# Grouped attention and a gated MLP on one core: V and U of batch 0 in one accumulation each, and a second order of the start-up's words

## The chip, the cores and the metric

One NeuronCore of a Trainium2 chip. The time is device microseconds of one launch. Each kernel is executed several times, and the median is given; one execution was profiled by the hardware profiler, and its trace is what the views are taken from.

## The reference

Eight batches; each is independent of the others but for the weights.

```python
# q 8x16x384x64, k and v 8x4x384x64 (four query heads share a k/v head)
attn = softmax(q @ k.T / 8) @ v            # by batch and head
x = attn, heads joined                      # 8 x 384 x 1024
h = relu(x @ w_in)                          # 1024 -> 1024
u, v = h[..., :512], h[..., 512:]
v = (v - mean(v)) / sqrt(var(v) + 1e-6)     # over the 512
v = w_spatial @ v + b_spatial               # over the 384 positions
out = (u * v) @ w_out                       # 512 -> 1024
```

## The kernel before

The work is cut into small steps, each with a short name, and the order of the steps is written out by hand as lists of words (RAMP, START, STEADY, LAST). A word is a step, its indices and its batch: in START a word without marks is batch 0, `+` is one batch on, `++` two, `+++` three; in STEADY and LAST `'` is one batch back. Each word issues its instructions on whatever engines they need, and every engine runs its own instructions strictly in the order in which the words issue them. So one list sets at once the order of TensorE (PE), VectorE (DVE), ScalarE (ACT), GpSimd (POOL) and of the DMA queues of SP and POOL. Waits between engines are put in by the framework from the buffers that are written and read.

By batch, the words are:

- **Loads** (SP's queue): `lk`, `lq0`, `lq1`, `lv` bring k, the two halves of q (768 KB each) and v in fp32. For batch 0 they are cut finer (`lqj`, `lqd`, `lkg`). The fp32 buffers are single (pool `ld`, one buffer by tag): a load of the next batch waits until the casts of the one before have read the buffer. `wv0`, `wv1`, `wu0`, `wu1` (L137) and `wo` (L144) load and convert the weights from POOL's queue; `wv` is the V half of w_in's columns, `wu` the U half, 0 and 1 the first and last four of its eight row blocks. `ws` (L150, L151) loads the spatial weight and bias, `cws` casts them on POOL (L157, L160), `tws` (L166) turns the weight by a DMA transpose.
- **Casts** to fp16: `ck`, `cq0`, `cq1`, `cv` on POOL (L184, L247, L197); in batch 0 also pieces on VectorE (`cqjv`, `cqv`, `ckv1`) and ScalarE (`cka0`).
- **Turns**: k and q, and later x, must lie with their head dimension on the partitions. In batches 0 and 1 `Q`, `K`, `Tp` do this on TensorE (L292, L278, L378) with a copy back by VectorE (L297, L283, L379); from batch 2 on (for x from batch 1 on) `tk`, `tq`, `T` are DMA transposes in SP's queue (L263, L269, L368).
- **Attention**: `s0` to `s17` are score products (two matmuls of 512 columns into a pair of PSUM banks, L315), `e0` to `e17` their exponentials on ScalarE (L329), `X` the products with v (24 matmuls, L342), `N` the division by the row sums (VectorE, L356, L357), which gives a half of an x tile (the half of the heads that X's first index names).
- **MLP**: `V` is the V half of x @ w_in for one tile of 128 positions (8 matmuls of 512, L113), then relu on VectorE (L434) into v_r; `S` its mean and variance (L447, L448), `rs` 1/sqrt on ScalarE (L452, L453), `vn` the normalised tiles (L461), `p` the spatial product (L113, bias added at L492), `U` the U half for 128 of its columns (8 matmuls of 384), gated at L505, `O` the output product with copy (L525) and store (L533).
- `w` and a number: so many matmuls of 128 columns on a cleared tile (L303), results unused.

PSUM has eight banks. A helper hands out the bank, or the even pair, that has been unused for longest, in the order of the words; a step that gets a bank still being read waits for that reader.

In batch 0 before the change, V and U are split in START. `A0` to `A2` multiply the first four row blocks of w_in (the first half of the heads) and VectorE copies the result to SBUF (L414); the later `V0` to `V2` multiply the last four, add the kept part (L436) and take the relu of the sum in SBUF (L437). `H0` to `H3` and `U0` to `U3` do the same for U (copy L423, add L503, gate L505 from the sum). All other batches do V and U in one accumulation of eight matmuls. `gate_v` and `gate_u` take the split branch only where a kept part exists.

START covers batch 0, most of batches 1 and 2 and the loads of batch 3. STEADY is played for batches 3 to 7, LAST ends the work.

Of the kernel before, what the change touches and what calls it, by code (L numbers as in the profile page):

```python
# [17 lines left out]
def kernel(  # L18
# [622 lines left out]
    def play(b, text):  # L641
# [8 lines left out]
    RAMP = """  # L650
        lqj00 lkga0 lqj01 lqd01 lt lkg1 lqd10 lv lqd11"""
    START = """
        w28 cqjv00 cka0 Qj00 w4 Ka0 w5 cqjv01 Qj01 w7 cqp011 wv0 cqv010 s0 s2 cv wv1 lk+ lq0+ Qh01 cqv100 ckv1
        cqv111 s1 e0 lq1+ ws s3 lv+ w9 s5 e2 ck+ e1 cqv101 s4 e5 e4 w6 cq0+ cqv110 s7 wu0 Q10 K1 cq1+ cws Q11
        s8 e7 e3 wu1 tws s10 lk++ s6 s9 e6 e8 lq0++ e10 X00 X01 e9 lq1++ lv++ N00 s11 N01 e11 s13 X02 e13 N02
        s12 cv+ Tp00 X10 wo e12 N10 Tp01 K0+ A0 Tp10 Q12 s14 e14 A1 V0 X11 Tp02 s15 N11 s16 K1+ A2 s17 e16
        Tp11 Q00+ S0 e15 e17 V1 X12 N12 s1+ Q10+ Q01+ Tp12 e1+ s0+ s9+ e0+ S1 e9+ s10+ ck++ H0 Q11+ Q02+ V2
        s2+ e10+ S2 e2+ s11+ rs s3+ e3+ H2 s4+ vn e11+ cq0++ H1 e4+ X00+ cq1++ tk++ N00+ p1 X10+ s5+ tq0++
        tq1++ N10+ T0+ p0 H3 e5+ U0 s12+ e12+ s7+ Q12+ U1 p2 s13+ s14+ e7+ p3 e13+ cv++ X01+ N01+ e14+ U3 s6+
        lk+++ U2 s17+ X11+ e17+ e6+ N11+ lq0+++ T1+ s8+ V0+ O4 e8+ X02+ N02+ s2++ S0+ e2++ lq1+++ s15+ O5 s0++  # L660
        e0++ s1++ O0 e15+ s16+ e16+ O2 lv+++ e1++ O1 V1+ O3 s11++ X12+ e11++ s9++ ck+++ e9++ N12+ T2+ S1+
        s10++ X00++ N00++ e10++ s14++ cq0+++ X10++ s3++ s5++ N10++ e5++ s4++ e4++ V2+ e3++ cq1+++ s13++ e14++
        tk+++ s12++ tq0+++ s8++ tq1+++ e13++ X01++ S2+ rs+ e12++ T0++ e8++ vn+ N01++ s7++ X11++ N11++ e7++ p1+
        p2+ p0+ V0++ cv+++ s15++ s17++ s6++ e6++ U0+ e15++ X02++ s16++ N02++ S0++ e17++ e16++ T1++ U1+"""
    STEADY = """
        s2 s1 e2 s0 e0 U2'' X12' p3'' N12' lq0+ cq0+ e1 lk+ s11 lq1+ e11 U3'' s9 tq0+ s10 s4 e9 e10 O0'' X00
        N00 ck+ V1' X10 S1' e4 s5 s3 T2' e5 lv+ e3 N10 O1'' V2' S2' s14 s13 s12 e13 T0 e12 O2'' O3'' X01 e14
# [45 lines left out]
```

## Time and profile before

| | before |
|---|---|
| median of 8 executions | 255.5 us (254.25 to 259.04) |
| the profiled execution | 255.13 us, span 253.0 us |
| TensorE busy | 237.0 us (94%), mean granted clock 0.993 |
| VectorE, ScalarE, POOL busy | 173.9, 143.6, 46.8 us |
| DMA | 47.2 MB, mean 187 GB/s |
| busy of PE / DVE / ACT / POOL, 20 to 30 us | 8.57 / 9.15 / 4.59 / 10.00 us |
| 30 to 40 us | 8.81 / 9.12 / 6.27 / 1.33 us |
| 40 to 50 us | 9.81 / 9.60 / 6.77 / 4.71 us |
| 50 to 60 us | 7.55 / 4.36 / 3.11 / 1.86 us |

The span is the profiled execution from its first to its last instruction; the execution's own time, 255.13, holds 2.1 us around it. Busy time counts an engine's instructions without its waits. The granted clock is the share of TensorE's full speed that the throttle allowed. The DMA share is the mean busy share of the core's 16 DMA engines; in a short window it can come out above 1. In a timeline each line is a run of equal instructions: start, length, engine, code line, operation, what it writes and reads, how many, and in brackets the idle time ahead of it with what ended it. SPq lines are the issue of a DMA by SP, not its transfer.

### The profile page before, as it was taken

How to read it: one execution, taken by the hardware profiler on the slowest of the kernel's cores; microseconds unless marked ns; L12 is line 12 of the kernel's file. 1: busy time of each engine (PE TensorE's matmuls, PEld its weight loads, DVE VectorE, ACT ScalarE, POOL GpSimd, SP SyncE). 2: the span in 40 equal slices, each digit the busy share in tenths (PEclk: the TensorE clock that was granted, in tenths of full speed). 3: DMA queues.
4: the chain of work that ended last, by engine and by line, in shares of the span. 5: the costliest groups of instructions: out<-in, count | busy, mean ns of one | idle time of the engine just before them, and what ended most of it. 6: DMA issues, size and time to landing. Idle time of an engine off the chain costs nothing.

```text
span 253.0 us, 5788 instructions
## 1 busy us (share of the span) xinstructions
PE 237.0 (94%) x2395; PEld 129.8 (51%) x2395; DVE 173.9 (69%) x350; ACT 143.6 (57%) x164; POOL 46.8 (18%) x72
## 2 busy tenths in 40 slices
PE   7779798969978999999999999999999999999993
PEld 6446345434535454464545554465446454565672
DVE  2538989936648557966677667775787677776963
ACT  3984476644576784856658466748485765800000
POOL 1718800704200151002310061003300000000000
PEclk9999999988999999999999999999999999999999
DMA  6999899999794994779968798789879126220354
GB/s 207 262 271 336 128 229 295 171 230 256 247 190 93 272 156 123 192 183 283 194 192 210 209 249 167 221 160 275 217 172 168 23 44 206 87 41 0 126 210 166
DMA packets 78042, 47.20 MB, mean 187 GB/s; under 512 B 47168, under 2 KB 74176, under 8 KB 78016
## 3 DMA queue, kind: packets, MB, share of 16 engines
q1 hardware_dynamic: 74880, 43.36, 67.7%
q0 software_dynamic: 2720, 3.15, 7.5%
q8 instruction: 18, 0.29, 0.5%
q10 hardware_dynamic: 416, 0.33, 0.4%
q14 instruction: 8, 0.07, 0.1%
HBM read 25.95 MB, written 12.58 MB: 152 GB/s over the span
## 4 chain that ended last, share of the span: by engine, by line
PE 83%; DVE 6%; DMA 5%; ACT 4%; issue 1%; SPq 0%; DVEq 0%; ACTq 0%
PE banks L113 57%; PE banks L315 13%; PE banks L342 12%; ACT aT L329 4%; DMA q<-in_q_dram 2%; DMA k<-in_k_dram 1%; DMA xT<-x 1%; DVE v_r L437 1%; DVE v_r L436 1%; DVE bn L447 1%; PE banks L292 1%; DVE q L247 1%; DVE gT L505 0%; PE banks L378 0%; DVE qT L297 0%
## 5 line engine op out<-in xcount | busy, mean ns | idle before, releaser
L329 ACT ACTIVATE aT<-banks 128x1024 f16<-128x1024 f32 x144 | 137.8, 1025 | 73.1 <-PE banks L315 66.9
L113 PE MATMUL banks<-w_in,xT 128*128 128x512 f16 x192 | 46.4, 384 | 4.0 <-DMA xT<-x 2.5
L113 PE MATMUL banks<-w_out,gT 128*128 128x512 f16 (+1 forms) x196 | 48.0, 381 | 0.0
L342 PEld LDWEIGHTS <-aT 128*128 128x128 f16 x1152 | 41.0, 98 | 13.3 <-ACT aT L329 5.9
L113 PE MATMUL banks<-xT,w_in 128*128 128x384 f16 (+1 forms) x320 | 47.3, 294 | 0.1
L315 PE MATMUL banks<-qT,kT 64*128 64x512 f16 x288 | 44.5, 381 | 2.2 <-ACT aT L329 0.6
L342 PE MATMUL banks<-v,aT 128*128 128x65 f16 x1152 | 43.4, 194 | 3.0 <-ACT aT L329 3.0
L247 POOL CAST q<-q 128x768 f16<-128x768 f32 (+1 forms) x29 | 23.6, 842 | 101.9 <-DMA q<-in_q_dram 65.6
L525 DVE COPY osb<-banks 128x512 f32<-128x512 f32 x47 | 32.0, 687 | 10.4 <-PE banks L113 9.9
L113 PEld LDWEIGHTS <-w_in 128*128 128x128 f16 x320 | 25.7, 98 | 17.7 <-issue 5.9
L357 DVE TENSOR_TENSOR x<-banks,rec 128x512 f16<-128x512 f32 x48 | 33.2, 691 | 1.7
L113 PEld LDWEIGHTS <-xT 128*128 128x128 f16 x192 | 18.1, 98 | 24.8 <-DMA xT<-x 3.0
L434 DVE TENSOR_SCALAR v_r<-banks 128x512 f32<-128x512 f32 x21 | 14.5, 691 | 23.0 <-PE banks L113 23.0
L113 PEld LDWEIGHTS <-gT 128*128 128x128 f16 x196 | 17.1, 99 | 24.9 <-issue 10.0
L315 PEld LDWEIGHTS <-kT 64*128 64x128 f16 x288 | 12.1, 94 | 24.8 <-issue 19.0
L505 DVE SCALAR_TENSOR_TENSOR gT<-banks,vs 128x384 f16<-128x384 f32 x24 | 13.4, 558 | 11.7 <-PE banks L113 11.7
L492 DVE TENSOR_TENSOR vs<-banks,bias_tp 128x384 f32<-128x384 f32 x28 | 14.9, 552 | 6.6 <-PE banks L113 6.6
L113 PE MATMUL banks<-wsT,v_n 128*128 128x384 f16 x96 | 19.3, 326 | 0.0
L447 DVE BATCH_NORM_STATS2 bn<-v_r 128x6 f32<-128x512 f32 x24 | 16.5, 689 | 0.4
L356 DVE RECIPROCAL rec<-banks 128x8 f32<-128x8 f32 x48 | 9.7, 202 | 9.1 <-PE banks L342 8.0
L461 DVE TENSOR_SCALAR v_n<-v_r,mv,rstd 128x512 f16<-128x512 f32 x24 | 11.6, 540 | 0.7 <-ACT rstd L453 0.6
L113 PEld LDWEIGHTS <-v_n 128*128 128x128 f16 x96 | 8.0, 98 | 6.2 <-issue 2.3
(49 smaller groups left out, 92.2 us busy)
## 6 DMA issues: line engine op xcount, KB each, us to landing
out_dram<-osb SPq DMA_DIRECT2D x22, 512.0 KB, 3.0
q<-in_q_dram SPq DMA_DIRECT2D x14, 768.0 KB, 8.1
v<-in_v_dram SPq DMA_DIRECT2D x8, 384.0 KB, 4.0
k<-in_k_dram SPq DMA_DIRECT2D x7, 384.0 KB, 6.4
w_in<-in_moe_w_in_dram POOLq DMA_DIRECT2D x8, 256.0 KB, 6.8
q<-in_q_dram SPq DMA_DIRECT2D x8, 192.0 KB, 4.2
w_out<-in_moe_w_out_dram POOLq DMA_DIRECT2D x2, 512.0 KB, 11.7
out_dram<-osb SPq DMA_DIRECT2D x3, 256.0 KB, 2.1
```

What stands on the lines that cost most here:

```text
L113: nc.tensor.matmul(dst[c : c + cols], w[:, c : c + cols], m, start=(i == 0), stop=(i == n - 1))
L247: engine(columns(b, gp, T["q16", b, gp])[:, js, :, half, :], T["q32", b, gp][:, half, js, :].rearrange("p j (t d) -> p j t d", t=NST),)
L315: nc.tensor.matmul(banks[:, xs[half], :], T["kT", b][lo:hi, t, gp, :], rhs[lo:hi, c * 512 : (c + 1) * 512], start=True, stop=True,)
L329: nc.scalar.activation(T["aT", b, gp, c][:, t, :, :], banks[:, x : y + 1 : y - x, :], AF.Exp, scale=scale)
L342: nc.tensor.matmul(banks[:, xs[half], j * (D + 1) : (j + 1) * (D + 1)], aT[:, t, half, o : o + P], T["v16", b][:, 2 * gp + half, t, 0 : D ...
L357: nc.vector.tensor_tensor(T["x16", b, tq][:, gp], ps[:, :, :, 0:D], rec.to_broadcast([P, 2, G, D]), ALU.mult)
L434: nc.vector.tensor_scalar(v_r, banks[:, x, :], 0.0, None, op0=ALU.max)
L447: nc.vector.bn_stats(bn, T["v_r", b, st])
L461: engine.tensor_scalar(v_n, T["v_r", b, st], T["mv", b][:, st, 0:1], T["rstd", b][:, st : st + 1], op0=ALU.subtract, op1=ALU.mult,)
L492: nc.vector.tensor_tensor(vs, f32(x, S), bias_tp, ALU.add)
L505: nc.vector.scalar_tensor_tensor(T["gT", b][:, mu, :], src, 0.0, T["vs", b, mu], op0=ALU.max, op1=ALU.mult)
L525: copy(osb[:, half * 512 : (half + 1) * 512], banks[:, x, :])
```

## The change

START is replaced. Its words are the same but for these: `A0` to `A2` and `H0` to `H3` are gone, so that `V0` to `V2` and `U0` to `U3` of batch 0 take the branch of one accumulation over eight row blocks; and there are 74 matmuls of the `w` words instead of 59. The order of the other words differs from just behind `s0` on, for all batches in START. SP's queue keeps its order up to the load of batch 3's first q half, and POOL's whole queue keeps its order; on TensorE, VectorE and ScalarE instructions change places. Among the moves: `ckv1`, the VectorE cast of the second half of batch 0's k, stands behind the copies of `Q10` and `Q11` and the four q casts on VectorE (before, behind the first of the four and ahead of the copies); `s0++` and `e0++` stand ahead of `V0+` (before, behind); `lq1+++` stands ahead of `T1+`, and `lv+++` ahead of the stores. Nothing else in the file changes; STEADY and LAST are the same.

```diff
--- before.py
+++ after.py
@@ -650,18 +650,18 @@
     RAMP = """
         lqj00 lkga0 lqj01 lqd01 lt lkg1 lqd10 lv lqd11"""
     START = """
-        w28 cqjv00 cka0 Qj00 w4 Ka0 w5 cqjv01 Qj01 w7 cqp011 wv0 cqv010 s0 s2 cv wv1 lk+ lq0+ Qh01 cqv100 ckv1
-        cqv111 s1 e0 lq1+ ws s3 lv+ w9 s5 e2 ck+ e1 cqv101 s4 e5 e4 w6 cq0+ cqv110 s7 wu0 Q10 K1 cq1+ cws Q11
-        s8 e7 e3 wu1 tws s10 lk++ s6 s9 e6 e8 lq0++ e10 X00 X01 e9 lq1++ lv++ N00 s11 N01 e11 s13 X02 e13 N02
-        s12 cv+ Tp00 X10 wo e12 N10 Tp01 K0+ A0 Tp10 Q12 s14 e14 A1 V0 X11 Tp02 s15 N11 s16 K1+ A2 s17 e16
-        Tp11 Q00+ S0 e15 e17 V1 X12 N12 s1+ Q10+ Q01+ Tp12 e1+ s0+ s9+ e0+ S1 e9+ s10+ ck++ H0 Q11+ Q02+ V2
-        s2+ e10+ S2 e2+ s11+ rs s3+ e3+ H2 s4+ vn e11+ cq0++ H1 e4+ X00+ cq1++ tk++ N00+ p1 X10+ s5+ tq0++
-        tq1++ N10+ T0+ p0 H3 e5+ U0 s12+ e12+ s7+ Q12+ U1 p2 s13+ s14+ e7+ p3 e13+ cv++ X01+ N01+ e14+ U3 s6+
-        lk+++ U2 s17+ X11+ e17+ e6+ N11+ lq0+++ T1+ s8+ V0+ O4 e8+ X02+ N02+ s2++ S0+ e2++ lq1+++ s15+ O5 s0++
-        e0++ s1++ O0 e15+ s16+ e16+ O2 lv+++ e1++ O1 V1+ O3 s11++ X12+ e11++ s9++ ck+++ e9++ N12+ T2+ S1+
-        s10++ X00++ N00++ e10++ s14++ cq0+++ X10++ s3++ s5++ N10++ e5++ s4++ e4++ V2+ e3++ cq1+++ s13++ e14++
-        tk+++ s12++ tq0+++ s8++ tq1+++ e13++ X01++ S2+ rs+ e12++ T0++ e8++ vn+ N01++ s7++ X11++ N11++ e7++ p1+
-        p2+ p0+ V0++ cv+++ s15++ s17++ s6++ e6++ U0+ e15++ X02++ s16++ N02++ S0++ e17++ e16++ T1++ U1+"""
+        w28 cqjv00 cka0 Qj00 w4 Ka0 w5 cqjv01 Qj01 w7 cqp011 wv0 cqv010 s0 cv e0 Qh01 s2 wv1 lk+ e2 s1 w10
+        cqv111 s4 cqv100 e1 cqv110 cqv101 s5 lq0+ lq1+ s3 s7 ws e3 w20 lv+ ck+ cq0+ e5 wu0 cq1+ Q10 e7 Q11
+        ckv1 s8 e4 e8 K1 cws s6 wu1 s9 tws lk++ s10 e6 X00 e10 e9 s11 X01 N00 N01 Tp00 X02 Q12 s13 N02 e11 X10
+        N10 lq0++ lq1++ Tp01 s12 lv++ K1+ s14 e12 K0+ Tp10 V0 cv+ e14 wo e13 Tp02 X11 N11 ck++ s17 s16 s15 e17
+        S0 Tp11 e15 e16 V1 Q00+ X12 N12 Q10+ s1+ s0+ Tp12 e1+ s9+ Q01+ S1 e9+ s10+ e0+ V2 S2 e10+ s2+ e2+ s3+
+        cq0++ Q11+ rs s11+ s4+ X00+ vn e11+ e4+ p1 e3+ cq1++ N00+ p0 tk++ X10+ s5+ Q02+ N10+ e5+ p2 U0 s12+
+        s7+ s14+ tq0++ p3 e7+ tq1++ U2 s13+ e12+ Q12+ cv++ T0+ s6+ lk+++ e14+ e6+ U3 U1 e13+ X01+ N01+ s17+
+        lq0+++ s8+ e17+ X11+ s0++ N11+ e8+ e0++ V0+ lq1+++ O2 T1+ X02+ N02+ O0 s1++ lv+++ s2++ s15+ e2++ e1++
+        O4 O5 s16+ e16+ O1 O3 ck+++ s11++ s9++ e15+ X12+ e11++ e9++ N12+ V1+ cq0+++ S0+ s10++ e10++ s5++ s3++
+        X10++ S1+ e5++ X00++ N10++ s4++ T2+ N00++ cq1+++ s14++ e14++ V2+ tk+++ S2+ s13++ s7++ e4++ e3++ s8++
+        e13++ rs+ s12++ X01++ tq0+++ vn+ tq1+++ e12++ T0++ X11++ e7++ s6++ N01++ e8++ p1+ N11++ p0+ U0+ e6++
+        V0++ s15++ e15++ cv+++ s16++ p2+ e16++ X02++ s17++ T1++ S0++ N02++ e17++ U1+"""
     STEADY = """
         s2 s1 e2 s0 e0 U2'' X12' p3'' N12' lq0+ cq0+ e1 lk+ s11 lq1+ e11 U3'' s9 tq0+ s10 s4 e9 e10 O0'' X00
         N00 ck+ V1' X10 S1' e4 s5 s3 T2' e5 lv+ e3 N10 O1'' V2' S2' s14 s13 s12 e13 T0 e12 O2'' O3'' X01 e14
```

## The prediction

> **What bounds the kernel now.** I read the windows first, to find where TensorE is short of work, then TensorE's timeline at the largest hole, then the queues behind that hole.
>
> Windows: length, busy time of PE, PEld, DVE, ACT and POOL with instruction counts, granted clock, DMA share, GB/s.
> ```profile
> 51.76:54.21 2.45, 0.00 (x1) 0.01 (x1) 0.81 (x2) 1.74 (x2) 0.00 (x0) 1.00 0.79 139
> 54.21:60.00 5.79, 5.79 (x41) 2.72 (x42) 1.86 (x4) 0.26 (x1) 1.86 (x3) 0.71 1.07 286
> ...
> 69.00:79.35 10.35, 7.90 (x119) 4.59 (x116) 6.19 (x15) 8.70 (x12) 0.00 (x0) 1.00 0.87 188
> 79.35:224.00 144.65, 144.65 (x1442) 76.84 (x1441) 101.81 (x201) 92.74 (x105) 19.57 (x28) 1.00 0.74 177
> ```
> From 79.35 us to 224 TensorE has no hole at all, and behind that comes a tail that the change does not touch. So the end moves by exactly what the start-up wins or loses ahead of 79 us. There TensorE is idle 2.45 us in one piece, runs the next 5.79 us at a mean clock of 0.71 (5.79 x 0.29 = 1.7 us lost), and lacks another 10.35 - 7.90 = 2.45 us between 69 and 79 us, where ScalarE is busy 8.70 of 10.35.
>
> TensorE's timeline at the hole:
> ```profile
> 51.37 0.39 PE L315 MATMUL banks<-qT,kT 64*128 64x512 f16 x2
> 54.21 2.62 PE L113 MATMUL banks<-w_in,xT 128*128 128x512 f16 x8 [2.45 <-DMA xT<-x]
> ```
> The waiting word is V0+; it needs T0+, the DMA transpose of batch 1's first x tile. I call its landing **the gate**. What holds T0+ is SP's queue (start, length):
> ```profile
> 9.03 0.37 SPq L178 DMA_DIRECT2D k<-in_k_dram  x1
> 9.50 2.82 SPq L223 DMA_DIRECT2D q<-in_q_dram  x2
> ...
> 46.34 4.63 SPq L269 DMA_TRANSPOSE qT<-q  x2
> 51.06 1.26 SPq L368 DMA_TRANSPOSE xT<-x  x1
> ```
> T0+ stands behind tq0++ and tq1++, which wait for POOL's casts, which wait for the loads of batch 2:
> ```profile
> 19.75 1.60 POOL L247 CAST q<-q 128x768 f16<-128x768 f32 x2 [4.18 <-DMA q<-in_q_dram]
> ...
> 44.33 1.98 POOL L247 CAST q<-q 128x768 f16<-128x768 f32 x2 [5.90 <-DMA q<-in_q_dram]
> 46.63 1.92 POOL L247 CAST q<-q 128x768 f16<-128x768 f32 x2 [0.33 <-DVE uparts L503]
> ```
> N10+, which T0+ needs too, ends at 43.3 us: VectorE is not what the gate waits for. From 2 us to 44 us the DMA share of the page's slices is 0.9 or more but for one.
>
> **The change, part by part.**
>
> *Half products gone.* Removed on VectorE: 3 copies L414 (0.69 us each), 3 adds L436 (0.69), 4 copies L423 (0.55), 4 adds L503 (0.55); three L437 (0.43, 0.43 and 1.92) become L434 at 0.69, and the one gT that took 1.22 becomes 0.56. Sum 2.07 + 2.07 + 2.2 + 2.2 + 2.78 - 2.07 + 0.66 = 9.9 us, all before 52 us. TensorE's 24 + 32 matmuls stay. TensorE idles only 1.29 + 0.15 + 0.58 + 0.68 = 2.7 us between 20 us and 51.4, so no more than that can be won here. The wait of 1.29 goes (it follows the L437 of 1.92, which stands beside a POOL cast):
> ```profile
> 25.27 1.92 DVE L437 TENSOR_SCALAR v_r<-v_r 128x512 f32<-128x512 f32 x1
> 27.11 0.40 DVE L379 COPY xT<-banks 128x512 f16<-128x512 f16 x1
> ```
> A new wait comes at p1: rstd (0.5) and v_norm (1.46) lie ahead of it and the only cover left is X00+ (0.85), the H words being gone: +1.1. With the rest gone and s0++ (0.3) put in, TensorE comes to V0+ at 51.76 - 2.7 + 1.1 + 0.3 = 50.5 us. It then waits for the gate. So this part is worth nothing by itself: what is late next is T0+. Bounds: -2.7 if the gate were open, 0 at worst, since up to 3 us of delay ahead of V0+ are covered by the wait.
>
> *Fifteen more idle matmuls* (59 to 74, about 0.07 us each by L303's 9 in 0.68): 1.0 us, ahead of the gate and largely in the holes of 0.42, 0.52 and 0.20 us that TensorE has between 10 and 12 us. Cost 0; without cover at most 1.0, still inside the wait.
>
> *The casts behind the gate.* cq0++ and cq1++ took 1.98 and 1.92 beside VectorE's L503 and L505 on uparts; alone they take 1.60 (the row at 19.75), and 0.33 of waiting stands between them. With uparts gone T0+ comes 0.38 + 0.32 + 0.33 = 1.0 us sooner, less what the DMA engines can't take: the windows from 46 to 54 us show DMA shares of 0.70, 1.29, 1.17 and 0.86, so there is room for most. I take -0.8; bounds -1.0 and 0.
>
> *ckv1 moved behind Q11: lk+ comes late.* This is the edit that the diff hides. The buffer of k is single: SP's load lk+ waits for ckv1, the VectorE cast of K's second half. Before, that cast ran at 8.51 and lk+ went out at 9.03. Now VectorE does first four q casts, of which the first waits for the load that lands at 10.60, then the copies of Q10 and Q11:
> ```profile
> 10.60 1.33 DVE L247 CAST q<-q 128x384 f16<-128x384 f32 x3 [1.64 <-DMA q<-in_q_dram]
> 12.38 0.42 DVE L297 COPY qT<-banks 128x512 f16<-128x512 f16 x1 [0.46 <-ACT aT L329]
> ```
> 10.60 + 4 x 0.44 = 12.4 (end of casts), + 0.5 to Q10's copy, + 2 x 0.33 for Q10 and Q11, + 0.45 for ckv1: lk+ at about 14.0, 5.0 us later. Behind it on SP stand lq0+, lq1+, ws, bias and lv+. Behind those, through q0+'s landing (19.75), hang in an unbroken row on POOL cq0+, wu0, cq1+, cws, then tws, the loads of batch 2, the casts and T0+. lq1+ loses less: it waited until 11.9 before for cqv101, and now goes out at 15.0. What may hide it are the other DMAs:
> ```profile
> 10.00:11.00 1.00, 0.56 (x6) 0.18 (x2) 0.40 (x1) 1.00 (x2) 1.00 (x2) 1.00 1.16 178
> 11.00:12.00 1.00, 0.30 (x3) 0.14 (x4) 0.93 (x3) 1.00 (x2) 0.74 (x2) 1.00 1.16 187
> ```
> In these two rows the engines are full at 180 GB/s, mostly with w_in (wv0, wv1: 4 x 256 KB; queue q0 moved 3.15 MB in 7.5% of 253 us, 166 GB/s). Of that 1.05 MB some 0.8 is left at 10.6 us (an estimate: begun near 8 us, at half of the engines until then): 4.9 us of full engines, to 15.5, just when lk+'s bytes begin. Then k+ and q0+ (1.18 MB) have the engines to themselves at the 320 GB/s of 6 to 8 us: 3.7 us, so q0+ lands near 19.2 instead of 19.75. I take 0. Bounds: -0.5 (as worked), and +4.5 if nothing useful fills the hole (lq0+ goes out 5.0 later, less 0.5).
> The Trainium skill ("DMA: Bandwidth & Descriptors", section on queues, rings and completion order) says that each DMA engine goes round the queue rows that have work. By that rule a late queue gives its share to the other one, and the sum stands with 0 here; by the upper bound the time would be 4.5 higher.
>
> *s0++ and its exp moved ahead of V0+.* Two matmuls, 0.25 us in the steady stretch (L315, 6 in 0.75), leave the path behind the gate: -0.25. They need tq0++, which lands about 50.5, before the gate. Their exp (0.94 us) runs in the wait, in which ScalarE stood still 6.24 us (53.5 to 59.7). Behind the gate ScalarE paces TensorE: 2.45 us of idle between 69 and 79 us. One exp less to do there, and X12+, V1+ put later among the scores: -0.9 of these 2.45. Bounds 0 and -2.45.
>
> *Order of O, s, X behind the gate, loads of batch 3*: lq1+++ now goes ahead of T1+, lv+++ ahead of the stores. V1+ stands later (before 64.4, now about 66), so T1+ has time; 0, bounds +/-0.5.
>
> *The clock.* A wait of 53.4 - 50.5 = 2.9 us in place of 2.45: I take the same 1.7 us loss; bounds -1.7 (none) and +1.7 (twice).
> The Trainium skill speaks against the change here ("TensorE: Matmul & The Clock Gate", part 1): an idle window of about 3.4 us halves the clock. The rows (0.71 after 2.45 us of idle) agree with one such window; a second one, by that rule, would add an estimated 1.7.
>
> **Sum**: -0.8 + 0 - 0.25 - 0.9 + 0 = -1.95 us. Against the profiled execution (span 253.0, time 255.13) 253.2; that execution lies 0.4 below the median of 255.5, which would give 253.6. I say **253.4**.
>
> **Rivals.**
> 1. *Slower: the late lk+ is not hidden.* If w_in alone does not fill the engines from 10.6 to 15 us, q0+ lands up to 4.5 later and the gate with it. For: an unbroken chain from 19.75 to T0+. Against: the 1.16 shares above. It decides from a landing 1.95 us later (21.7) on; at 4.5: 253.4 + 4.5 = 257.9, less about 0.5 for lq1+'s smaller delay, 257.4.
> 2. *No change: the gate stays.* The DMA engines can't take the transposes sooner, or batch 2's loads lose what the casts win, and ScalarE lags as before. For: share 1.29 at 48 to 50 us. Left: -0.25, and 255.0.
> 3. *The wait no longer costs the clock*: split by s0++, or shorter. 253.4 - 1.7 = 251.7.
> That TensorE's new order is itself short of work until 52 us is covered by the wait up to 2.9 us.
>
> **Chances.** Forecast 0.47, rival 1 0.23, rival 2 0.18, rival 3 0.12. About 0.3% (0.8 us) is what a measurement of this kernel can tell from no change. Faster by more than that: 0.47 + 0.12 = 0.59; within: 0.18; slower: 0.23. Range: rival 3 with 0.8 more (both upper gains), 250.9, to rival 1's 257.0, which leaves out part of rival 1 and extremes.
>
> **What would show it.** After: lk+ on SP near 14; q0+'s cast on POOL near 19.5 (21.7 or later: rival 1); casts of batch 2 at 1.6; T0+ near 50.2, and V0+ starting near 53.4 behind a wait of 2 to 3 us; one stretch at half clock; less than 2 us idle between there and the steady stretch. The prediction is wrong if TensorE's largest wait is not at V0+, or lies behind 56 us.

## The result, and the profile after

| | before | after |
|---|---|---|
| median | 256.64 us (57 executions, 253.63 to 259.11) | 257.91 us (20 executions, 255.56 to 259.43) |
| profiled execution | 255.13 us, span 253.0 | 257.69 us, span 255.7 |
| VectorE busy | 173.9 us | 165.2 us |
| mean granted clock | 0.993 | 0.993 |

The ratio of the times is 1.0088, 95% interval 1.0065 to 1.0112: the change makes the kernel 0.9% slower, where 0.8% faster was predicted. Ratios here and below leave out the executions that lie over 1.5% above the fastest of their kernel, so they differ from the quotients of the medians shown (here 257.91 / 256.64 = 1.005). The old kernel, executed beside the experiments, had medians of 256.88 us (runs 1 to 4), 256.51 (5 to 8) and 256.44 (9 to 12). The forecast of 253.4 us stood on a median of 255.5 over 8 executions; of the 4.5 us between 253.4 and 257.91, 1.1 lie in that base.

First the windows of the changed kernel (length, busy time of PE, PEld, DVE, ACT, POOL with counts, clock, DMA share, GB/s):

```profile
53.08:55.75 2.67, 0.00 (x1) 0.01 (x1) 0.00 (x0) 1.02 (x1) 0.00 (x0) 0.97 0.81 149
55.75:61.63 5.88, 5.88 (x41) 2.60 (x42) 2.11 (x4) 0.00 (x0) 2.04 (x3) 0.72 1.03 323
69.00:81.00 12.00, 9.78 (x132) 5.54 (x131) 7.79 (x18) 9.25 (x12) 0.00 (x0) 1.00 0.79 157
81.00:181.00 100.00, 100.00 (x1000) 52.96 (x998) 69.44 (x138) 63.63 (x72) 18.70 (x27) 1.00 0.84 202
181.00:190.00 9.00, 7.40 (x60) 3.14 (x58) 5.81 (x12) 4.55 (x8) 0.82 (x1) 1.00 0.66 162
```

The shape of the start-up is as before: a hole of 2.67 us ahead of V0+, then 5.88 us at clock 0.72 (1.65 us lost), then 12.00 - 9.78 = 2.22 us of holes. Two things are worse. The gate lies later, and the fifth row has a hole of 1.60 us far behind the start-up, where the old kernel's profile had none. TensorE's timeline names both:

```profile
52.69 0.39 PE L315 MATMUL banks<-qT,kT 64*128 64x512 f16 x2 [1.99 <-DMA qT<-q]
55.75 3.49 PE L113 MATMUL banks<-w_in,xT 128*128 128x512 f16 x8 [2.67 <-DMA xT<-x]
...
183.09 1.90 PE L113 MATMUL banks<-w_in,xT 128*128 128x512 f16 x8 [1.60 <-DMA xT<-x]
```

V0+ starts 55.75 - 54.21 = 1.54 us later. The steady hole is V2', the V product of the third x tile of a batch, waiting for its DMA transpose T2'. What is behind V0+ without the clock and the steady hole is 255.7 - 55.75 - 1.65 - 1.60 = 196.7 us, against 253.0 - 54.21 - 1.7 = 197.1 before. So the two profiles differ by +1.54 (gate) + 1.60 (steady hole) - 0.4 (behind the gate) = 2.7 us, which is the difference of the spans.

Back from the gate: VectorE and then SP, POOL.

```profile
11.40 1.60 DVE L247 CAST q<-q 128x384 f16<-128x384 f32 x4 [3.32 <-DMA q<-in_q_dram]
13.56 0.76 DVE L297 COPY qT<-banks 128x512 f16<-128x512 f16 x2 [0.57 <-PE banks L292]
14.24 0.41 DVE L184 CAST k<-k 128x384 f16<-128x384 f32 x1
```
```profile
14.72 0.37 SPq L178 DMA_DIRECT2D k<-in_k_dram  x1
15.20 1.18 SPq L223 DMA_DIRECT2D q<-in_q_dram  x2
...
47.55 4.98 SPq L269 DMA_TRANSPOSE qT<-q  x2
52.62 1.26 SPq L368 DMA_TRANSPOSE xT<-x  x1
```
```profile
21.46 1.60 POOL L247 CAST q<-q 128x768 f16<-128x768 f32 x2 [1.68 <-DMA q<-in_q_dram]
...
45.92 1.60 POOL L247 CAST q<-q 128x768 f16<-128x768 f32 x2 [4.17 <-DMA q<-in_q_dram]
48.27 1.60 POOL L247 CAST q<-q 128x768 f16<-128x768 f32 x2 [0.75 <-DMA q<-in_q_dram]
```

lk+ goes out at 14.72 behind ckv1 (9.03 before), q0+'s cast starts at 21.46 (19.75), and all behind it is later by about as much. The casts of batch 2 take 1.60 us each, as worked out, yet the second now waits 0.75 us for its own load: what the casts won, the load took.

### The profile page after: what moved, and what is told of

Same layout as the page of the kernel before. It is cut to its first block, busy times and chain, and to the rows that moved or that the text cites. A ratio compares the mean times of both kernels' runs of the same rounds, so it can differ in the third digit from the quotient of the medians.

```text
span 255.7 us, 5785 instructions
## 1 busy us (share of the span) xinstructions
PE 237.0 (93%) x2410; PEld 130.8 (51%) x2410; DVE 165.2 (65%) x336; ACT 143.7 (56%) x164; POOL 45.9 (18%) x72
## 4 chain that ended last, share of the span: by engine, by line
PE 71%; DMA 16%; POOL 4%; DVE 3%; ACT 2%; SPq 2%; issue 1%; DVEq 0%; POOLq 0%
PE banks L113 51%; DMA q<-in_q_dram 12%; PE banks L315 10%; PE banks L342 9%; DMA xT<-x 3%; POOL q L247 2%; ACT aT L329 2%; DMA k<-in_k_dram 1%; DVE x L357 1%; SPq L269 1%; POOL setup L157 1%; DVE q L247 1%; POOL w_in L137 1%; DVE bn L447 0%; DVE v_n L461 0%
## 5 line engine op out<-in xcount | busy, mean ns | idle before, releaser
L113 PE MATMUL banks<-w_in,xT 128*128 128x512 f16 x192 | 47.0, 389 | 4.7 <-DMA xT<-x 4.3
L113 PE MATMUL banks<-w_out,gT 128*128 128x512 f16 (+1 forms) x196 | 46.9, 376 | 0.0
L113 PE MATMUL banks<-xT,w_in 128*128 128x384 f16 (+1 forms) x320 | 46.6, 294 | 0.0
L315 PE MATMUL banks<-qT,kT 64*128 64x512 f16 x288 | 43.3, 381 | 3.2 <-DMA qT<-q 2.0
L247 POOL CAST q<-q 128x768 f16<-128x768 f32 (+1 forms) x29 | 22.9, 817 | 100.1 <-DMA q<-in_q_dram 56.7
L434 DVE TENSOR_SCALAR v_r<-banks 128x512 f32<-128x512 f32 x24 | 16.6, 692 | 31.0 <-PE banks L113 31.0
L505 DVE SCALAR_TENSOR_TENSOR gT<-banks,vs 128x384 f16<-128x384 f32 x28 | 15.6, 557 | 13.5 <-PE banks L113 13.4
```

What stands on the lines that cost most here:

```text
L113: nc.tensor.matmul(dst[c : c + cols], w[:, c : c + cols], m, start=(i == 0), stop=(i == n - 1))
L247: engine(columns(b, gp, T["q16", b, gp])[:, js, :, half, :], T["q32", b, gp][:, half, js, :].rearrange("p j (t d) -> p j t d", t=NST),)
L315: nc.tensor.matmul(banks[:, xs[half], :], T["kT", b][lo:hi, t, gp, :], rhs[lo:hi, c * 512 : (c + 1) * 512], start=True, stop=True,)
L434: nc.vector.tensor_scalar(v_r, banks[:, x, :], 0.0, None, op0=ALU.max)
L505: nc.vector.scalar_tensor_tensor(T["gT", b][:, mu, :], src, 0.0, T["vs", b, mu], op0=ALU.max, op1=ALU.mult)
```

## The experiments

Two theories stood against each other at first, and a third was formed on the profiles of the changed kernel and the first four runs (it stands in run 7's expectation). *Late k load*: ckv1's move delays lk+ and with it the gate. *Clock*: the wait at the gate costs what it does through the half clock, and it varies. *Steady stretch*: the new order also loses time behind 80 us, where T2' stands on SP behind tq0+, which waits for a POOL cast and that for a load, just as T0+ does at the gate. A rival to all of them is the removal of the half products itself. The expectations were written before each run and name theories by letters of their own.

**1. ckv1 put back, in the changed kernel.**
```diff
-  s1 w10 cqv111 ... e7 Q11 ckv1 s8
+  s1 ckv1 w10 cqv111 ... e7 Q11 s8
```


> The new order with one word moved: the VectorE cast of K's second half back ahead of the four q casts. Theory L (the late load moved the gate): batch 1's k load leaves SP near 9 us instead of 14.7, the cast of q0+ on POOL starts near 19.7 instead of 21.5, T0+ goes out near 50.5 to 51 instead of 52.6, and the time falls by 1.5 to 3.3 us against the changed kernel, to the time of before or up to 1 us under it. Theory O (the new order of scores and products is itself the loss): the load leaves early as well, but the time falls by less than 0.7 us.

Measured: 257.96 us, ratio 1.0064 (1.0026 to 1.0102). lk+ went out at 8.63 and q0+'s cast started at 20.25, so V0+ came at 54.59, 1.16 us sooner than in the changed kernel's profile; but the ratio fell by only 0.24%, which the interval does not tell from nothing. A late lk+ is at most a part of the loss.

**2. ckv1 put late, in the old kernel.**
```diff
-  cqv100 ckv1 cqv111 ... Q10 K1 cq1+ cws Q11 s8
+  cqv100 cqv111 ... Q10 cq1+ cws Q11 ckv1 K1 s8
```


> The old order with two words moved: the cast of K's second half and the turn of it behind the copies of Q10 and Q11, as in the new order; half products stay. Theory L: the k load of batch 1 leaves SP near 13.7 us, q0+'s cast starts 1 to 2 us later than 19.75, V0+ starts 1 to 2 us later than 54.2, and the time rises by 1 to 3 us. Theory O: the time stays within 0.7 us of before.

Measured: 256.61 us, ratio 0.9961 (0.9914 to 1.0007): not slower. Its profile does show a late landing, on POOL:

```profile
20.64 0.82 POOL L184 CAST k<-k 128x768 f16<-128x768 f32 x1 [8.51 <-DMA k<-in_k_dram]
22.95 1.60 POOL L247 CAST q<-q 128x768 f16<-128x768 f32 x2 [1.48 <-DMA q<-in_q_dram]
```

and V0+ at 57.95. That execution took 258.69 us, 2 us more than the kernel's median. One profile of a start-up with this much queueing is not the kernel's mean.

**3. One accumulation alone, in the old kernel.**
```diff
-  A0 A1 A2 H0 H1 H2 H3   (each removed from its place in START, nothing else moved)
```


> The old order with only the half products taken out: V and U of batch 0 in one accumulation each at the places of the later halves. VectorE loses about 9.9 us of work before 52 us. Theory L, and the recorded working: T0+ goes out 0.5 to 1 us sooner since POOL's casts are undisturbed, the wait at V0+ stays or grows, and the time is 0 to 1.5 us under before. Theory O says the half products filled holes of TensorE that nothing fills now: TensorE comes to V0+ later than 54 us, and the time rises by over 1 us.

Measured: 256.33 us, ratio 1.0021 (0.9977 to 1.0066). Taking the half products away is worth nothing that can be measured, and costs nothing. The loss comes with the order.

**4. The wait filled with idle matmuls, in the changed kernel.**
```diff
-  X11+ s0++ N11+ e8+ e0++ V0+
+  X11+ w28 s0++ N11+ e8+ e0++ w38 V0+
```


> The new order with 28 idle matmuls ahead of s0++ and 38 ahead of V0+, which fill most of the two waits of 1.99 and 2.67 us with matmuls whose results are unused. V0+ can't start sooner, since its transpose lands when it did. Theory C (a good part of the loss is the clock that falls to half after the waits): the granted clock stays at 1.0 between 54 and 62 us, V0+ and the product behind it take 1.7 to 2 us less together, and the time falls by 1.5 to 2.5 us against the changed kernel. If the clock is not what the waits cost: the time is the same or up to 1 us longer, the fillers being in the way.

Measured: 254.69 us, ratio 0.9926 (0.9895 to 0.9957). TensorE's timeline:

```profile
52.29 0.39 PE L315 MATMUL banks<-qT,kT 64*128 64x512 f16 x2 [0.78 <-DMA qT<-q]
52.62 2.30 PE L303 MATMUL banks<-warm 128*128 128x128 f16 x38
55.45 1.90 PE L113 MATMUL banks<-w_in,xT 128*128 128x512 f16 x8 [0.53 <-DMA xT<-x]
```

V0+ starts 0.3 us sooner than in the changed kernel, yet takes 1.90 us instead of 3.49: the clock stays. The fall, 3.2 us by the medians, is more than the 1.5 to 2.5 expected. The mean loss to the clock, (1 - clock) x span over all executions, is 0.66 us here and 3.62 us in the changed kernel (21 executions). The wait itself remains; the half clock behind it was 3 us of the time. In the old kernel's 81 executions beside the experiments that loss is 3.1 us on average (2.8 over the 55 that the ratios count), so the clock explains some 0.5 to 0.8 us of the difference between the orders.

**5. The same in the old kernel.**
```diff
-  T1+ s8+ V0+ O4
+  T1+ s8+ w34 V0+ O4
```


> The old order with 34 idle matmuls ahead of V0+, so that the wait of 2.45 us is nearly full of matmuls. V0+ starts when it did. Theory C: the granted clock stays at 1.0 behind the wait, and the time falls by 1.5 to 3.5 us against before, as it did for the new order; the new order with its wait filled should then still be about 1.4 us slower than this one (the difference that is left between the two kernels when the time lost to the clock is taken off). If before does not lose to the clock as the new order does, it falls by less than 1 us.

Measured: 259.06 us, ratio 1.0122 (1.0066 to 1.0179), a miss. Its timeline:

```profile
52.22 2.07 PE L303 MATMUL banks<-warm 128*128 128x128 f16 x34
56.69 3.33 PE L113 MATMUL banks<-w_in,xT 128*128 128x512 f16 x8 [2.39 <-DMA xT<-x]
```

The gate came at 56.69, 2.5 us later than in the old kernel's profile, so that 34 matmuls covered only half of the hole and 2.39 us of idle halved the clock again. q0+'s cast started at 22.11 with lk+ out at 9.04, as early as ever. The fill stands 30 us behind that cast, so it can't be its cause; what moved the landing is open. Nor is it one odd execution: all six took 257.42 to 260.07 us. Why this version is slower than the old kernel is not shown.

**6. T0+ ahead of tq0++ and tq1++, in the old kernel.** It takes the gate away by another way: T0+ needs only N10+, which ends at 43.3 us.
```diff
-  s5+ tq0++ tq1++ N10+ T0+ p0
+  s5+ N10+ T0+ tq0++ tq1++ p0
```


> The old order with one word moved on SP's queue alone: T0+ ahead of tq0++ and tq1++ instead of behind them. Its x tile is ready at 43.3 us. Theory G (both kernels lose their start-up time at the gate: T0+'s landing, and the halved clock that follows the wait): T0+ goes out near 45 us, V0+ starts near 51.5 to 52 without a wait for a DMA, the granted clock stays at 1.0 there, and the time falls by 3 to 5 us against before. If the gate were covered by something else, the time would fall by less than 1 us.

Measured: 252.28 us, ratio 0.9865 (0.9823 to 0.9907). SP's queue, then TensorE:

```profile
47.46 2.07 SPq L368 DMA_TRANSPOSE xT<-x  x1
49.58 4.52 SPq L269 DMA_TRANSPOSE qT<-q  x2
```
```profile
53.22 1.90 PE L113 MATMUL banks<-w_in,xT 128*128 128x512 f16 x8 [1.77 <-DMA xT<-x]
```

A wait of 1.77 us is left, and V0+ behind it runs at full clock (1.90 us). This holds although q0+'s cast was late in this profile as well (21.81).

**7. The same in the changed kernel** (V0+ goes ahead of s0++, whose qT now comes later).
```diff
-  Q02+ N10+ e5+ p2 ... cv++ T0+ s6+ ... X11+ s0++ N11+ e8+ e0++ V0+
+  Q02+ N10+ T0+ e5+ p2 ... cv++ s6+ ... X11+ N11+ e8+ V0+ s0++ e0++
```


> The new order with T0+ ahead of tq0++ and tq1++, and V0+ ahead of s0++ and e0++, since s0++ needs tq0++. The late k load stays. Theory G: with the gate out of the way nothing of the new order's loss is left; V0+ starts near 51 us with no wait, and the time is that of the old order with the same edit, within 1 us. Theory W (the new order loses in the steady stretch too, where V waits for the third x tile's transpose: 1.60 us in its profile, none in that of before): it stays 1 us or more above the old order with the same edit.

Measured: 255.08 us, ratio 0.9969 (0.9921 to 1.0016); V0+ at 51.67 behind a wait of 1.48, but a new wait of 1.50 us at V1+ (64.07) and one of 1.94 us at 179.69 in the steady stretch.

**8. As 7, with ckv1 put back as in 1.**

> As the run before, and the cast of K's second half ahead of the q casts, so that the k load of batch 1 leaves SP near 9 us. Theory G: the loads no longer matter once T0+ does not stand behind them; within 0.7 us of the run with T0+ alone. Theory L in a wider form (late loads cost also elsewhere): 1 to 2 us less than that run.

Measured: 254.18 us, ratio 0.9962 (0.9922 to 1.0002): the same as 7. V0+ started at 52.18, sooner than in run 6, though still behind 2.33 us of waiting and at a lowered clock (it took 2.57 us). So with T0+ and lk+ early in both orders the changed one was still 1.0% behind the old one (0.9962 against 0.9865). Neither the late load nor the gate could be the whole cause. The profile again had steady waits for xT, 0.35 us at 151.81 and 1.62 at 180.87. In the five profiles of the old order so far (before, 2, 3, 5, 6) such waits sum to 0, 0, 0.33, 2.04 and 0 us, mean 0.5; in the five of the new one (after, 1, 4, 7, 8) to 1.60, 1.86, 0.74, 1.94 and 1.97, mean 1.6. Both play the same STEADY list.

**9. T2' ahead of tq0+ in STEADY, in the changed kernel.** Only SP's queue changes.
```diff
-  lq1+ e11 U3'' s9 tq0+ ... s3 T2' e5
+  lq1+ T2' e11 U3'' s9 tq0+ ... s3 e5
```


> The changed kernel with one more move, in the steady words of batches 3 to 7: T2' (the transposes of the third x tile) goes to SP ahead of tq0+ instead of behind it; the start-up is the changed kernel's. Theory W (the new order loses some 1.1 us more than the old one in the steady stretch, because T2' stands on SP behind tq0+, which waits for POOL's cast of a q load that has just landed): no wait of a V word for xT longer than 0.3 us between 80 and 190 us, against 1.60 in the changed kernel's profile; ratio to the old kernel 1.0025 (0.6 % less than the changed kernel's 1.009). Theory G (all of the loss lies ahead of the gate, and what stands in the steady stretch is chance of one execution): ratio stays at 1.007 to 1.010. Theory Q (T2' ahead takes DMA time from the transposes of q, and s words wait in its place): a wait for qT over 0.5 us in the steady stretch and a ratio over 1.009.

Measured: 256.14 us, ratio 1.0031 (0.9996 to 1.0066), 0.57% less than the changed kernel; theory W's number, though the interval just touches the changed kernel's (from 1.0065 on). The mean loss to the clock, 3.56 us, is what it was (3.62), so the clock is not what won. SP's queue at the place of the hole, first in the changed kernel, then in this one:

```profile
176.18 1.41 SPq L269 DMA_TRANSPOSE qT<-q  x1
177.69 1.59 SPq L368 DMA_TRANSPOSE xT<-x  x1
```
```profile
174.67 1.23 SPq L368 DMA_TRANSPOSE xT<-x  x1
176.36 2.41 SPq L269 DMA_TRANSPOSE qT<-q  x1
```

and the V2' that it feeds here, on TensorE, without a wait in brackets:

```profile
181.19 1.89 PE L113 MATMUL banks<-w_in,xT 128*128 128x512 f16 x8
```

The three transposes of xT issued between 166 and 190 us (how many, median us from issue to landing), in the old and in the changed kernel:

```profile
xT<-x SPq DMA_TRANSPOSE x3, 3.4
```
```profile
xT<-x SPq DMA_TRANSPOSE x3, 4.2
```

The one that V2' waits for in the changed kernel took 5.4 us.

The windows from 80 to 190 us, the changed kernel's and this one's, show what that leaves of the holes, 0.12 us of 1.72 (of these 1.60 at V2'):

```profile
80.00:190.00 110.00, 108.28 (x1063) 56.68 (x1062) 75.51 (x150) 69.18 (x80) 19.52 (x28) 1.00 0.82 197
```
```profile
80.00:190.00 110.00, 109.88 (x1072) 57.70 (x1071) 77.48 (x153) 71.14 (x82) 19.52 (x28) 1.00 0.81 201
```

There is no room for a wait for qT of over 0.5 us either: theory Q is out.

**10. The same in the old kernel.**

> The old kernel with the same move of T2' alone. Theory W: the old order's steady stretch had waits of 0, 0, 0.3, 0 and 2.0 us in the five profiles with that order, mean 0.5, so 0.2 % to win at most: ratio 0.998 to 1.000. Theory G: 1.000. Theory Q: over 1.000, with waits for qT.

Measured: 256.23 us, ratio 0.9999 (0.9961 to 1.0037). The old order gains nothing by it, so the steady loss, as far as medians show it, belongs to the new order (run 5's profile shows that the old one can have such waits too).

**11. T0+ and T2' early, in the old kernel.**

> The old kernel with T0+ ahead of tq0++ and tq1++ in the start-up (252.28 us in an earlier run, ratio 0.9865) and T2' ahead of tq0+ in the steady words. Theory W: 0.9845 to 0.9865, no steady waits. Theory G: 0.9865. Theory Q: over 0.988.

Measured: 252.81 us, ratio 0.9851 (0.9806 to 0.9896), like 6; TensorE is busy 110.00 of the 110 us from 80 to 190.

**12. T0+, T2' and ckv1 early, in the changed kernel.**

> The changed kernel with three moves: ckv1 back ahead of Q11, T0+ ahead of tq0++ and tq1++ (with V0+ ahead of s0++), T2' ahead of tq0+ in the steady words. Its start-up alone gave 254.18 us, ratio 0.9962, and its profile had 0.35 + 1.62 us of steady waits. Theory W: those go, ratio 0.989, and what is left between it and the old kernel with the same two moves of T words is under 0.3 %. Theory G: stays at 0.996, 1 % above the old kernel with the same moves; then the new order has a cost that is neither the late k load, nor the gate, nor the steady waits.

Measured: 251.88 us, ratio 0.9821 (0.9778 to 0.9863), better than theory W asked, and again 110.00 of 110 us from 80 to 190. V0+ at 50.90 behind 1.24 us, at full clock:

```profile
50.90 1.90 PE L113 MATMUL banks<-w_in,xT 128*128 128x512 f16 x8 [1.24 <-DMA xT<-x]
```

The table that decides (ratios to the old kernel; in the last two rows the changed order has ckv1 early as well):

| | old order | changed order | difference |
|---|---|---|---|
| as it stands | 1 | 1.0088 | +0.9% |
| T2' early | 0.9999 | 1.0031 | +0.3%, intervals overlap |
| T0+ early | 0.9865 | 0.9962 | +1.0% |
| T0+ and T2' early | 0.9851 | 0.9821 | -0.3%, intervals overlap |

By the medians given with each run the four differences are +0.5%, 0.0%, +0.8% and -0.4%. In both pairs T2' takes away most of the difference: 0.57% with T0+ where it was, 1.4% with T0+ early, against 0.01% and 0.14% in the old order. The first figure is at the edge of the noise, the second clear of it. But 1.4% is more than run 8's steady waits (1.97 us, 0.8%): its profile also lost clock at V0+, ahead of every steady word, where run 12's did not, and by the medians the two versions are 2.3 us apart. So it is shown that the steady wait is the larger part of the loss; its exact size is not. Once T2' no longer stands behind tq0+, the two orders can't be told apart. Versions 6, 11 and 12 beat both kernels, by 1.35% to 1.8%; among them the intervals do not choose.

## Why the prediction was wrong

- **"So the end moves by exactly what the start-up wins or loses ahead of 79 us" failed**, and by the ratios it is the step that cost the most (0.57 of 0.88%). It was read from one profile of the old order, in which TensorE has no hole behind 79 us. No hole is not the same as slack. V2' starts 12.8 us behind the issue of lq0+ where it does not wait, T2' is issued 8.9 to 9.5 us behind it in the last three rounds of the two kernels, and where no wait follows it takes 3.1 to 3.8 us to land: it lands about when it is needed. In those rounds of the old order's five profiles and of the new one's five, the cast that frees tq0+ starts on average 5.7 and 6.1 us behind lq0+'s issue, yet T2' is issued 9.2 us behind it in both; what differs is how long it takes. The seven waits of 0.7 us and more (five in the new order, two in the old, both in run 5) stand behind transposes that landed 4.3 to 5.4 us after their issue; the other 23 landed in 3.1 to 3.8, with waits of at most 0.35. Issued ahead of tq0+ (runs 9 to 12), T2' goes out 6.3 us behind lq0+ and is in time even when it takes 5.3 us. The wait was worth 0.57% of 255 us, 1.5 us (1.60 in the profile). Why more of these transposes land late in the new order is open: START's tail differs in many places, and no run took it apart.
- **"ckv1 moved behind Q11 ... I take 0"** was low for the profile. lk+ went out at 14.72 (predicted 14.0, the casts began at 11.40 instead of 10.60), and q0+'s cast at 21.46 where 19.5 was expected: rival 1's mechanism, short of its deciding 21.7. It moved the gate of this execution by up to 1.54 us: V0+ was to start near 53.4 and started at 55.75, which in the one profile is a larger miss than the steady hole. But the 54.21 that the prediction started from was early for the old order (54.88 in run 3's profile, 56.69 in run 5's), and the new order's other gates with T0+ in its place came at 54.59 to 55.77 (runs 1, 4 and 9), so a later gate is not shown for the order as such. On medians its price is smaller than can be measured: 0.24% less when undone (run 1), no loss when done alone (run 2). In nine profiles with an early lk+ the cast starts at 19.75 to 22.11 us (mean 20.8), in five with a late one at 21.06 to 22.95 (mean 21.8): a shift of 1.0 us within spreads of 2.4 and 1.9. Rival 1's time (257.4) was close to the result, but by a cause that explains the smaller part.
- **The casts: -0.8 taken, -0.13 found.** From lk++'s issue to T0+'s it is 52.62 - 29.36 = 23.26 us, against 51.06 - 27.67 = 23.39. The casts did become 1.60 us; the second then waited 0.75 us for batch 2's load. The stall that went uncovered a transfer.
- **ScalarE's lag: -0.9 taken, about -0.2 found** (holes of 2.22 us, 2.45 before). With s0++ ahead of V0+ (-0.25 taken) the gain behind the gate is the 0.4 us worked out above, of 1.15 expected.
- **The clock: the same loss, right** (1.65 us for 1.7), and the wait at V0+ was rightly put at 2 to 3 us. A second wait, 1.99 us at s0++, was not foreseen: tq0++ was to land about 50.5, and s0++ could start only at 52.69. What the clock term misses is the size over executions: 3.1 to 3.6 us on average, not one stretch of 1.7 us.
- **"This part is worth nothing by itself", of the half products, was right**: run 3, where VectorE did get 8.7 us of work less (165.2 us busy; 9.9 less was worked out). So was the point at which TensorE runs out of work: 50.2 us predicted without s0++; the last product ahead of s0++ ends at 49.78 + 0.91 = 50.7.
- V0+'s wait behind 56 us, named as what would show the prediction wrong, did not come (55.75). All the signs named lay in the start-up, so none could warn of the steady stretch.

The sum, put right by the runs: 255.13 + 1.54 + 1.60 - 0.4 = 257.9 for a profiled execution that took 257.69.

## What to carry to other kernels

Before costing a change in a start-up, measure the slack of the steady stretch behind it, not only its holes: how long ahead of its use each transfer lands. A transfer that is ready to go should not stand in an in-order DMA queue behind one that waits for a load and a cast; two such moves here (T0+, T2') are worth more than the whole change, and with them (and ckv1 early) the loss that the change brought can't be seen any more. And where a difference is under 1%, settle it by pairs of runs with the same edit in both orders, since a profile is one execution of many.

## What the runs showed of the hardware

- Idle time and clock at V0+: waits of 1.24 and 1.77 us left V0+ at 1.90 us (full clock); 2.33 us made it 2.57, 2.39 made it 3.33, 2.67 made it 3.49. The stretch behind ran at 0.73 for 6.32 us after the 2.33, at 0.72 for 5.88 us after the 2.67. A wait of 1.94 us at V2' (run 7) left it at 1.90 too. So in these runs the loss begins between 1.94 and 2.33 us of idle. It can be larger: after 3.16 us (run 3) the next 5.92 us ran at 0.54.
- The Trainium skill ("TensorE: Matmul & The Clock Gate", part 1) puts the idle window at about 3.4 us and calls it free-running. The runs here lose the clock after shorter idle, 2.33 us.
- Idle matmuls in the wait keep the clock: 254.69 us instead of 257.91, with the wait no shorter. They must cover it: with 2.39 us left uncovered (run 5) nothing was kept.
- A load issued at the same place of the same queue lands at quite different times: q0+'s cast started between 19.75 and 22.11 us in the nine profiles in which lk+ went out between 8.6 and 9.2.
- A DMA transpose of the same size, issued at the same place of its queue, landed 3.1 to 5.4 us after its issue (T2' in the last three steady rounds of the ten profiles in which it stands behind tq0+).
